# Reordering the first loads of a fused long-convolution and gated-GLU kernel, and fetching D once

## The chip, the cores and the metric

The kernel runs on one core of one Trainium2 chip. The metric is device time in microseconds (us) of one launch; the runs shown are the median of three. Profiles are of one execution on the chip. PE is TensorE's matmul, PEld its weight load, DVE is VectorE, ACT is ScalarE, POOL is GpSimd and SP is SyncE, whose queue issues nearly all DMAs here.

## The reference

x is 2048 tokens by 640 channels in bf16. It is normalised over the channels and goes into two branches that are added to x.

```python
def _A_ref(q, k, v, shift_k, ssm_k, ssm_D):        # q = layernorm(x)
    k_shift = sum over t<4 of k_pad[:, t:t+S, :] * shift_k[:, 3 - t]
    kv = k_shift * v
    y = irfft2(rfft2(kv padded to 2S) * rfft2(ssm_k padded to 2S))[:S]   # causal convolution, 2048 taps
    y = y + kv * ssm_D
    return q * y

def _B_ref(x, w_gate, w_up, w_down):               # x = layernorm(x), F = 1728
    h = sigmoid(x @ w_gate) * (x @ w_up)
    return h @ w_down

x = A_q; xn = _layernorm(x)
return x + _A_ref(xn, A_k, A_v, A_shift_k, A_ssm_k, A_ssm_D) + _B_ref(xn, B_w_gate, B_w_up, B_w_down)
```

## The kernel before

**Branch B** goes over four groups t of 512 tokens. For each, 13 tiles of 128 gate columns and 13 of up columns (`product`, L271), one shared tile for the last 64 columns of each (L292), then the down product (L315) over 14 tiles of hidden rows, in eight pieces of 128 tokens by 320 columns, each in two parts of seven hidden tiles. ACT takes the sigmoid (L280), DVE multiplies (L286) and adds the down product to x (L320). Group 0 is normalised and turned at the very start; its first two gate and up tiles run in quarters (L262).

**Branch A** goes over five chunks c of 128 channels. DVE makes kv from k, the four taps and v (`kv_op`, L348 to L357, in two halves of eight instructions) and turns the filter h with a 32 by 32 transpose (`h_turn`, L334, two instructions a chunk). POOL adds D to the filter's first tap (`add_D`, L328), so that D is part of the convolution. Stage 1 (`st1_mm`, L374 and L376) multiplies kv and h with the table S1 on TensorE; ACT moves the product out of PSUM and SP writes it to DRAM (L392), from where it is read back in another arrangement (L409) for stage 2 (L418), the product of the spectra (L431, L433), and the two inverse stages (L447, L488). DVE multiplies with xn (`inv2_q`, L493, into the tile yx) and adds to x (L498).

**Groups 1 to 3 of x** are normalised while the rest runs: statistics by DVE (`ln_norms`, L200 and L204), the power -1/2 by POOL (L212), then xn by DVE (L217) or ACT (L229), and four DMA transposes by SP (`xn_turn`, L250).

**What sets the order.** Nothing is scheduled automatically after the setup. Each kind of step is a chain of calls, and the string `ORDER` names, letter by letter, which chain makes its next call; so every engine has a fixed list that it works through in order. SP's list begins with the chain "m", a tuple of loads, which the change reorders. Its loads are `load_w` (gate and up columns lo to hi, L177 and L180), `load_wd` (down weights by hidden tile, L186), `ks(c)` (halo and two halves of a chunk's k, L163, L164 and L159), `hs(c)` (`load_h`: D for the chunk, L140, and the filter in four pieces, L143), `vs(c)` (two halves of v, L173), `load_taps` (the tile sraw, L147) and `load_x(1)` (group 1 of x, L133). The table S1 is loaded behind the down weights.

The tile hn that holds a chunk's filter has one buffer: the loads of chunk 1's filter wait until both L334 of chunk 0 have read it. The tile dr for D also has one buffer, so its next load waits for POOL's L328. k has two buffers (`kxs`). Besides what the data need, SP's instruction list has each DMA wait for the landing of an earlier one: completions are counted on eight semaphores in turn, and an issue waits for the DMA that used its semaphore last.

Of the kernel before, what the change touches and what calls it, by code (L numbers as in the profile page):

```python
# [10 lines left out]
BF16 = mybir.dt.bfloat16  # L11
# [3 lines left out]
ALU = mybir.AluOpType  # L15

S = 2048
DM = 640
FF = 1728
P = 128  # L20
# [37 lines left out]
def kernel(  # L58
# [14 lines left out]
    nc = tc.nc  # L73
# [6 lines left out]
    Drow = A_ssm_D.rearrange("(o d) -> o d", o=1)  # L80
# [7 lines left out]
    res = ctx.enter_context(tc.tile_pool(name="res", bufs=1))  # L88
    cv = ctx.enter_context(tc.tile_pool(name="cv", bufs=1))
    dr = ctx.enter_context(tc.tile_pool(name="dr", bufs=1, space=bass.MemoryType.DRAM))  # L90
# [7 lines left out]
    S1t = res.tile([P, NB, 2, P], U16, name="S1t")  # L98
    TBt = res.tile([P, 2, NB, P], U16, name="TBt")
    SMt = res.tile([P, 3, 32], U16, name="SMt")  # L100
    S1 = S1t.bitcast(BF16)
    TB = TBt.bitcast(BF16)
    SM = SMt.bitcast(BF16)
# [21 lines left out]
    sync = nc.sync  # L125
# [3 lines left out]
    cin = [dict() for _ in range(NC)]  # L129
# [5 lines left out]
    def load_h(c):  # L135

        d = cin[c]
        d["hn"] = cv.tile([P, 4, 512], BF16, name="hn")
        d["dr"] = cv.tile([1, P], BF16, name="dr")
        sync.dma_start(d["dr"][:, :], Drow[:, c * P:(c + 1) * P])  # L140
        for q in range(4):
            src = A_ssm_k[c * P:(c + 1) * P, 512 * q:512 * q + 512].rearrange("(k r) t -> r k t", k=4)
            sync.dma_start(d["hn"][32 * q:32 * q + 32, :, :], src)  # L143

    def load_taps(c):
        cin[c]["sraw"] = cv.tile([P, 4 * P], BF16, name="sraw")
        sync.dma_start(cin[c]["sraw"][:], srow[:, 4 * c * P:4 * (c + 1) * P].to_broadcast((P, 4 * P)))  # L147

    def taps(c):
# [175 lines left out]

    def add_D(c):
        h0 = cin[c]["kvh"][0:1, 1, 0:2, :].rearrange("p b c -> p (b c)").rearrange("p (c e) -> p e c", e=2)[:, 0, :]
        nc.gpsimd.tensor_tensor(h0, h0, cin[c]["dr"][:, :], ALU.add)  # L328

    def h_turn(c, n):  # L330

# [27 lines left out]
    chunks = [dict() for _ in range(NC)]  # L359
# [6 lines left out]
    def st1_mm(c, n):  # L366
# [5 lines left out]
        for i in range(4):  # L372
            b = 4 * n4 + i
            nc.tensor.matmul(ps[:, i, 0:P], lhsT=S1[:, b, h, :], rhs=cin[c]["kvh"][:, 0, b, :], start=True, stop=True)  # L374
            hp = cin[c]["kvh"][:, 1, :, :].rearrange("p b c -> p (b c)").rearrange("p (b c e) -> p b e c", b=8, e=2)
            nc.tensor.matmul(ps[:, i, P:2 * P], lhsT=S1[:, b, h, :], rhs=hp[:, b // 2, b % 2, :], start=True, stop=True)  # L376

# [21 lines left out]
    def rd2(s):  # L399
# [5 lines left out]
        else:  # L405
            t2 = (xn[:, 12:NB, :].rearrange("p b d -> p (b d)")[:, 0:2048] if at == 2 else
                  S1[:, 8 * at:8 * at + 8, :, :].rearrange("p b h k -> p (b h k)")).rearrange("p (r e) -> p r e", r=8)
        src = chunks[c]["d1"].rearrange("(r q) h b e -> r (q h b) e", q=NQ)
# [60 lines left out]
    def rdb(c, n):  # L469
# [4 lines left out]
        elif c and n == 1:  # L474
            bi = S1[:, 8:NB, :, :].rearrange("p (h b) s c -> p h (b s) c", h=2)
        else:
# [12 lines left out]
                                 start=(h == 0), stop=(h == 1))  # L489

    def inv2_q(c, m):
        chunks[c]["yx", m] = yx = cv.tile([P, 4, P], BF16, name="yx")
        nc.vector.tensor_tensor(yx[:, :, :], chunks[c]["pb", m][:, :, :], xn[:, 4 * m:4 * m + 4, c * P:(c + 1) * P],  # L493
                                ALU.mult)

# [35 lines left out]
    for i in range(4):  # L531
        m = 3 if i < 3 else NC
# [15 lines left out]
    def step(k, fn, *args):  # L548
        chains[k].append((fn, args))
# [16 lines left out]
    def hs(c):  # L566
        return [(load_h, c)]

    def ks(c):
        return [(load_halo, c), (load_k, c, 0, 8), (load_k, c, 8, NB)]  # L570

    def vs(c):
        return [(load_v, c, 0, 8), (load_v, c, 8, NB)]

    for k in ((load_w, sync, 512, 1024, 0),
              (load_w, sync, 512, 1024, 1),
              (load_taps, 0),
              (sync.dma_start, SMt[:], SMd.ap()),
              (load_w, sync, 1024, 1280, 0),
              (load_w, sync, 1024, 1280, 1),  # L580
              (load_wd, sync, 0, 7),
              *ks(0),
              (load_w, sync, 1280, FF, 0),
              (load_w, sync, 1280, FF, 1),
              *hs(0),
              *vs(0),
              (load_wd, sync, 7, NFC),
              (sync.dma_start, S1t[:], S1d.ap()),
              *hs(1),
              (load_x, sync, 1),  # L590
              *ks(1),
              *vs(1)):
        step("m", *k)
# [4 lines left out]
    for c in range(NC):  # L598
        for n in range(2):
            step("H", h_turn, c, n)  # L600
        step("D", add_D, c)
        for n in range(8):
            step("a", st1_mm, c, n)
# [17 lines left out]
        for m in range(4):  # L621
            step("d", inv2_mm, c, m)
            step("q", inv2_q, c, m)
            step("q", inv2_x, c, m)
        for n in range(16):
            step("k", kv_op, c, n)
        if c == 0:
            continue
        step("T", load_taps, c)
        step("t", taps, c)  # L630
        if c > 1:
# [73 lines left out]
```

## Time and profile before

| | us |
|---|---|
| median of 3 runs (lowest, highest) | 234.59 (233.74, 235.59) |
| the profiled execution: time | 234.78 |
| its span, first to last instruction | 233.0 |
| PE busy | 227.5 (98%) |
| PEld busy | 130.9 (56%) |
| DVE busy | 203.4 (87%) |
| ACT busy | 123.5 (53%) |
| POOL busy | 12.4 (5%) |
| granted TensorE clock | 1.00 |
| DMA | 56.79 MB, mean 244 GB/s |

The span is read from the first to the last instruction; the time of the execution holds 1.78 us more around it. Busy times are sums over the whole span; where an engine waits, and for what, is read from the stretches, the chain of waits and the timeline, which the prediction shows.

### The profile page before, as it was taken

How to read it: one execution, taken by the hardware profiler on the slowest of the kernel's cores; microseconds unless marked ns; L12 is line 12 of the kernel's file. 1: busy time of each engine (PE TensorE's matmuls, PEld its weight loads, DVE VectorE, ACT ScalarE, POOL GpSimd, SP SyncE). 2: the span in 40 equal slices, each digit the busy share in tenths (PEclk: the TensorE clock that was granted, in tenths of full speed). 3: DMA queues.
4: the chain of work that ended last, by engine and by line, in shares of the span. 5: the costliest groups of instructions: out<-in, count | busy, mean ns of one | idle time of the engine just before them, and what ended most of it. 6: DMA issues, size and time to landing. Idle time of an engine off the chain costs nothing.

```text
span 233.0 us, 5431 instructions
## 1 busy us (share of the span) xinstructions
PE 227.5 (98%) x2199; PEld 130.9 (56%) x2200; DVE 203.4 (87%) x357; ACT 123.5 (53%) x158; POOL 12.4 (5%) x26
## 2 busy tenths in 40 slices
PE   7999999997999999999999999999999999999995
PEld 2844446776454555677554544478654544446772
DVE  5444899799999999999999999997799999997773
ACT  2533321676364887765675847674556667752000
POOL 5210010040001100000011000000000000000000
PEclk9999999999999999999999999999999999999999
DMA  6999999896999969999989899689989999364884
GB/s 199 325 329 208 267 317 294 208 266 143 330 221 303 299 221 242 263 223 230 329 237 277 224 319 272 184 217 190 269 210 311 279 263 254 117 169 117 220 266 136
DMA packets 96159, 56.79 MB, mean 244 GB/s; under 512 B 55878, under 2 KB 90374, under 8 KB 95878
## 3 DMA queue, kind: packets, MB, share of 16 engines
q1 hardware_dynamic: 95702, 56.03, 92.6%
q10 hardware_dynamic: 432, 0.41, 0.5%
q8 instruction: 17, 0.28, 0.5%
q14 instruction: 8, 0.07, 0.1%
HBM read 36.12 MB, written 18.35 MB: 234 GB/s over the span
## 4 chain that ended last, share of the span: by engine, by line
PE 87%; DVE 5%; DMA 4%; issue 1%; SPq 1%; ACT 0%; DVEq 0%
PE pu L271 22%; PE pg L271 22%; PE pd L315 21%; PE psb L488 4%; DMA x<-in_A_q_dram 4%; PE ps L374 3%; PE ps L376 3%; PE ps L418 3%; PE psa L447 2%; PE idle L514 2%; PE pg L292 1%; DVE st L200 1%; PE pg L262 1%; PE pu L262 1%; DVE acc L354 1%
## 5 line engine op out<-in xcount | busy, mean ns | idle before, releaser
L271 PEld LDWEIGHTS <-w 128*128 128x128 bf16 x500 | 46.7, 98 | 53.9 <-issue 4.3
L315 PE MATMUL pd<-wd,hT 128*128 128x320 bf16 (+2 forms) x447 | 65.9, 299 | 0.1
L271 PE MATMUL pu<-xnT,w 128*128 128x512 bf16 x250 | 62.2, 379 | 0.0
L271 PE MATMUL pg<-xnT,w 128*128 128x512 bf16 x250 | 62.2, 379 | 0.0
L315 PEld LDWEIGHTS <-hT 128*128 128x128 bf16 x448 | 41.7, 98 | 18.2 <-issue 2.4
L280 ACT ACTIVATE sig<-pg 128x512 bf16<-128x512 f32 x52 | 31.1, 601 | 30.5 <-PE pg L271 23.8
L286 DVE TENSOR_TENSOR hT<-sig,pu 128x512 bf16<-128x512 bf16 x52 | 35.0, 682 | 10.8 <-PE pu L271 6.9
L232 ACT CAST xz<-ps 128x1024 bf16<-128x1024 f32 x36 | 35.1, 1014 | 15.5 <-PE ps L418 15.5
L232 ACT CAST t<-ps 128x1024 bf16<-128x1024 f32 x24 | 23.8, 1012 | 16.7 <-PE ps L376 14.5
L433 DVE TENSOR_TENSOR xz<-xz 128x2048 bf16<-128x2048 bf16 x20 | 24.4, 1221 | 0.2
L374 PE MATMUL ps<-kvh,S1t 128*128 128x128 bf16 x160 | 21.5, 218 | 1.2 <-DVE kvh L357 1.2
L376 PE MATMUL ps<-kvh,S1t 128*128 128x128 bf16 x160 | 21.6, 220 | 0.0
L354 DVE TENSOR_TENSOR acc<-acc,tmp 128x1024 bf16<-128x1024 bf16 x30 | 20.5, 684 | 0.3
L352 DVE TENSOR_TENSOR tmp<-kx,sc 128x1024 bf16<-128x1024 bf16 x30 | 20.5, 682 | 0.3
L320 DVE TENSOR_TENSOR x<-pd,x 128x320 bf16<-128x320 f32 (+2 forms) x32 | 15.2, 484 | 3.8 <-PE pd L315 3.6
L374 PEld LDWEIGHTS <-S1t 128*128 128x128 bf16 x160 | 15.5, 97 | 3.9 <-DVE kvh L357 1.4
L376 PEld LDWEIGHTS <-S1t 128*128 128x128 bf16 x160 | 15.4, 96 | 2.7 <-issue 0.2
L200 DVE BATCH_NORM_STATS2 st<-x 128x6 f32<-128x320 bf16 x32 | 13.8, 473 | 2.3 <-DMA x<-in_A_q_dram 2.3
L232 ACT CAST TBt<-ps 128x1024 bf16<-128x1024 f32 x14 | 13.8, 1012 | 2.7 <-PE ps L376 2.7
L493 DVE TENSOR_TENSOR yx<-psb,xn 128x512 bf16<-128x512 f32 x20 | 13.7, 687 | 1.4 <-PE psb L488 0.8
L431 DVE STREAM_SHUFFLE xz<-xz 128x512 f32<-128x512 f32 x20 | 14.6, 729 | 0.0
L232 ACT CAST ao<-psa 128x1024 bf16<-128x1024 f32 x9 | 9.0, 1013 | 8.6 <-PE psa L447 6.9
(56 smaller groups left out, 159.2 us busy)
## 6 DMA issues: line engine op xcount, KB each, us to landing
t<-d SPq DMA_DIRECT2D x15, 512.0 KB, 6.0
d<-t SPq DMA_DIRECT2D x13, 512.0 KB, 4.1
d<-TBt SPq DMA_DIRECT2D x7, 512.0 KB, 5.9
d<-ao SPq DMA_DIRECT2D x6, 512.0 KB, 5.5
bi<-d SPq DMA_DIRECT2D x6, 512.0 KB, 5.4
kx<-in_A_k_dram SPq DMA_DIRECT2D x10, 256.0 KB, 5.8
hn<-in_A_ssm_k_dram SPq DMA_DIRECT2D x20, 128.0 KB, 5.0
kvh<-in_A_v_dram SPq DMA_DIRECT2D x10, 256.0 KB, 5.2
```

What stands on the lines that cost most here:

```text
L200: nc.vector.bn_stats(st[:, i, SD * s2:SD * s2 + SD], x[:, b, s2 * 320:(s2 + 1) * 320])
L232: nc.scalar.copy(out=out, in_=in_)
L271: nc.tensor.matmul(pg[:, :], lhsT=w[:, c, u * UP + fc * P:u * UP + (fc + 1) * P], rhs=xnT[:, :, c, :], start=(c == 0), stop=(c == NC - 1))
L280: nc.scalar.activation(sig[fc][:, :], pgs[0, fc][:, :], ACT.Sigmoid)
L286: nc.vector.tensor_tensor(hT[:, fc, :], sig[fc][:, :], pgs[1, fc][:, :], ALU.mult)
L315: nc.tensor.matmul(pd[:, :], lhsT=hT[:, fc, bb * P:(bb + 1) * P], rhs=wd[:, fc, es], start=(fc == 0), stop=(fc == NFC - 1))
L320: nc.vector.tensor_tensor(x[:, 4 * t + bb, es], pds[bb, half][:, :], x[:, 4 * t + bb, es], ALU.add)
L352: nc.vector.tensor_tensor(d["tmp"][:, :, :], kx[:, lo + 3 - m:hi + 3 - m, :], sb(m), ALU.mult)
L354: nc.vector.tensor_tensor(d["acc"][:, :, :], d["acc"][:, :, :], d["tmp"][:, :, :], ALU.add)
L374: nc.tensor.matmul(ps[:, i, 0:P], lhsT=S1[:, b, h, :], rhs=cin[c]["kvh"][:, 0, b, :], start=True, stop=True)
L376: nc.tensor.matmul(ps[:, i, P:2 * P], lhsT=S1[:, b, h, :], rhs=hp[:, b // 2, b % 2, :], start=True, stop=True)
L433: nc.vector.tensor_tensor(z[:, 1:3, :, :], z[:, 0:1, :, :].to_broadcast((P, 2, 8, P)), z[:, 1:3, :, :], ALU.mult)
```

## The change

In the chain "m" of SP's loads three things move:

- chunk 0's k (`ks(0)`) goes from behind the first down weights to ahead of the gate and up columns 1024 to 1280;
- the down weights of hidden tiles 0 to 6 go from ahead of k to behind chunk 0's v, next to the other down weights;
- group 1 of x goes ahead of chunk 1's filter loads.

D is loaded once, as one row of 640 values in a tile of its own, ahead of chunk 0's filter, instead of 128 values for each chunk. The tiles sraw and yx share one buffer by a common tag. `ORDER` is the same, and so are all instructions of PE, DVE, ACT and POOL, apart from the tile from which L328 reads D.

```diff
@@ tiles
+    Dt = res.tile([1, DM], BF16, name="Dt")
@@ load_h(c)
         d = cin[c]
+        if c == 0:
+            sync.dma_start(Dt[:, :], Drow[:, :])
         d["hn"] = cv.tile([P, 4, 512], BF16, name="hn")
-        d["dr"] = cv.tile([1, P], BF16, name="dr")
-        sync.dma_start(d["dr"][:, :], Drow[:, c * P:(c + 1) * P])
@@ load_taps(c)
-        cin[c]["sraw"] = cv.tile([P, 4 * P], BF16, name="sraw")
+        cin[c]["sraw"] = cv.tile([P, 4 * P], BF16, name="sraw", tag="sy")
@@ add_D(c)
-        nc.gpsimd.tensor_tensor(h0, h0, cin[c]["dr"][:, :], ALU.add)
+        nc.gpsimd.tensor_tensor(h0, h0, Dt[:, c * P:(c + 1) * P], ALU.add)
@@ inv2_q(c, m)
-        chunks[c]["yx", m] = yx = cv.tile([P, 4, P], BF16, name="yx")
+        chunks[c]["yx", m] = yx = cv.tile([P, 4, P], BF16, name="yx", tag="sy")
@@ chain "m"
               (load_w, sync, 512, 1024, 1),
               (load_taps, 0),
               (sync.dma_start, SMt[:], SMd.ap()),
+              *ks(0),
               (load_w, sync, 1024, 1280, 0),
               (load_w, sync, 1024, 1280, 1),
-              (load_wd, sync, 0, 7),
-              *ks(0),
               (load_w, sync, 1280, FF, 0),
               (load_w, sync, 1280, FF, 1),
               *hs(0),
               *vs(0),
+              (load_wd, sync, 0, 7),
               (load_wd, sync, 7, NFC),
               (sync.dma_start, S1t[:], S1d.ap()),
+              (load_x, sync, 1),
               *hs(1),
-              (load_x, sync, 1),
               *ks(1),
               *vs(1)):
```

## The prediction

> **What bounds the kernel now.** I read first the busy times of the engines in a few long stretches, to find where TensorE stands still, then the chain that ended last around that place, and last the DMA side of it.
>
> The engines' busy time by stretch (stretch, its length, then busy time and instruction count of PE, PEld, DVE, ACT, POOL, the granted clock, the DMA share, GB/s):
>
> ```profile
> 0.00:1.17 1.17, 0.00 (x0) 0.00 (x0) 0.30 (x3) 0.01 (x1) 0.64 (x7) 1.00 0.00 0
> 1.17:54.00 52.83, 52.68 (x389) 31.62 (x389) 38.41 (x74) 21.78 (x34) 7.94 (x15) 1.00 1.06 270
> 54.00:55.24 1.24, 0.04 (x1) 0.00 (x1) 1.21 (x3) 1.01 (x1) 0.00 (x0) 1.00 0.84 161
> 55.24:226.00 170.76, 170.76 (x1781) 96.95 (x1782) 160.31 (x273) 100.65 (x123) 3.83 (x5) 1.00 0.93 242
> 226.00:233.00 7.00, 4.05 (x33) 2.28 (x31) 3.13 (x7) 0.00 (x0) 0.00 (x0) 1.00 0.44 134
> ```
>
> TensorE bounds it, at clock 1.00. Between its first matmul and the drain it is idle once, for 1.20 us just before 55.24; after that it is busy for 170.76 of 170.76 us, in an order fixed at build time. So the end moves one for one with the matmul at 55.24, and a reordering of the first loads can save 1.20 us at the very most.
>
> The chain that ended last (start, length, what), thinned, in order of time:
>
> ```profile
> 31.15 0.65 DVE kvh L357
> ...
> 33.67 0.33 SPq L143
> 34.05 0.42 SPq L143
> ...
> 35.46 8.80 DMA x<-in_A_q_dram
> ...
> 44.29 0.90 DVE st L200 x2
> ...
> 54.49 0.70 DVE kvh L357
> ...
> 55.24 0.23 PE ps L374
> ```
>
> The matmul at 55.24 is chunk 1's first stage-1 product. It waits for DVE's L357, and DVE works without a gap from 44.29 to there: 10.95 us, set off by group 1's x, which was issued at 35.46 and landed at 44.26. x stood behind the four h loads of L143, which SP may issue only when DVE has read chunk 0's h out of the buffer (33.65).
>
> What DVE itself does there (start, length, instruction, idle time before it and what ended it):
>
> ```profile
> 41.15 0.48 DVE L320 TENSOR_TENSOR x<-pd,x 128x320 bf16<-128x320 f32 x1
> 42.79 1.11 DVE L334 STREAM_TRANSPOSE kvh<-hn 128x512 f32<-128x512 f32 x1 [1.15 <-DMA hn<-in_A_ssm_k_dram]
> 44.29 0.49 DVE L200 BATCH_NORM_STATS2 st<-x 128x6 f32<-128x320 bf16 x1 [0.39 <-DMA x<-in_A_q_dram]
> ```
>
> DVE's order is fixed: **h first (L334), then x (L200)**. It was free at 41.64, waited 1.15 us for h and 0.39 us for x: 1.54 us of waiting, more than TensorE's 1.20.
>
> **The change part by part.**
>
> *k and the first down weights.* SP's list has chunk 0's k (two halo loads and two halves, 84 + 11.2 + 2 x 256 KB in the table of issues, whose KB are 1,024 bytes: 622 thousand bytes) ahead of the gate/up columns 1024 to 1280, and the down weights of tiles 0 to 6 behind chunk 0's v. DMA bytes up to S1 stay the same. k moves at the rate of these rows (same columns):
>
> ```profile
> 18.00:21.00 3.00, 3.00 (x15) 1.36 (x14) 0.80 (x2) 0.77 (x2) 0.00 (x0) 1.00 1.26 227
> 21.00:23.00 2.00, 2.00 (x11) 0.88 (x10) 1.43 (x3) 0.60 (x1) 0.00 (x0) 1.00 0.53 116
> 23.00:26.00 3.00, 3.00 (x15) 1.35 (x14) 2.43 (x5) 0.60 (x1) 0.00 (x0) 1.00 1.16 345
> ```
>
> At 227 GB/s that is 2.7 us. The gate columns of 1024 to 1280 were issued at 8.45 and landed 7.9 us later, at 16.35; they come to about 19.1, the up columns to some 20.2. TensorE reads them from its ninth gate tile on: tiles 2, 3, ... start at 11.98 and every 2.16 us, so tile 8 at 24.9. Margin 5.8 us: cost 0. Without that cover, each us late there would stop TensorE for one. Columns 1280 and up, chunk 0's h and v gain what the 1.147 MB of down weights took (3.3 us at 345 GB/s); DVE reads k first at 22.14, after 0.57 us of waiting for it. That wait goes, but at 25.20 DVE waits 0.57 us for TensorE's up tile anyway, so nothing is left of it: 0. The down weights 0 to 6 are read at 36.80. S1, which follows all down weights, landed at 39.95 (issue at 29.85, 10.1 to landing) and takes 1.049 MB / 395 GB/s (the rate of 33 to 36) = 2.7 us; so tiles 7 to 13 are in by 37.3 at the latest, and are read at 38.7; tiles 0 to 6 come 1.065 MB, 2.7 us at that rate, sooner, by 34.6. Cover 2.2 us, cost 0. S1 itself is read at 40.6 against 39.95: 0.6 us of cover, the thinnest; lateness beyond it first eats the 1.20 us that TensorE loses later anyway. Cost 0.
>
> *x ahead of chunk 1's h.* x no longer waits for DVE's 33.65: it is issued right behind S1, from about 30.4. The four h issues still wait for 33.65 and now follow x in the queue, then the taps. The same 1.18 MB of x and h move behind the same S1; only their order is turned, and the one that DVE reads first now comes last. Bound above: the pair ends when it ends today, 44.27. Then L334 starts 0.11 later at 44.38, takes 1.11, and L200 starts at 45.5 instead of 44.29: +1.2 us. Bound below: the pair is in before DVE is free at 41.64; then L200 starts at 42.75, 1.54 sooner, of which TensorE can use 1.20: -1.2. What lies between: h landed at 42.68 today (issue at 34.98, 7.7 to landing), x 1.6 us behind. If h holds today's time though x is ahead of it, L334 keeps 42.79, the 0.39 us wait for x goes, and the gain is 0.4. Two rows speak for a landing before 44.27: the DMA share fell to 0.53 in 21 to 23, so 2.0 x 0.47 = 0.94 us of queue time was lost behind k, which may not recur with other loads there; and h moved slowly (242 GB/s in 36 to 39, beside the tail of S1) where S1 alone had 395. Against: in 41 to 44.3 the mean rate was only 181 GB/s while x still was not in, so a few slow engines of the 16 set the landing, and these need not have lost the 0.94. I take half of the way between 42.68 and 44.27, moved up a little by the last point: h at 43.5. Then L334 at 43.6, L200 at 44.7: **+0.4 us**.
>
> A rule stands beside this. The Trainium skill, DMA: Bandwidth & Descriptors, section "Queues, rings and completion order", says that each DMA engine takes the descriptors of one ring in ring order; what is put ahead on SP's queue is thus paid in full by what is behind. The trace agrees in that x, behind h, landed 1.6 us after it. Strictly by that rule the sum would be the +1.2 of the upper bound, not +0.4.
>
> *Work behind it.* The four statistics feed POOL's L212, L223, L224, then ACT's two L229 (50.46) and SP's four transposes (50.39 to 55.6), read by the gate tile at 58.22. They move with DVE; so does TensorE: 0. k of chunk 1 (L163, L164, L159) is held by the landings of loads eight places ahead in SP's list. The halo no longer waits 2.7 us for S1, but the first half now waits for x to land: from 40.90 to about 42; it took 4.7 us to land, so 46.7, and DVE reads it at 48.34. Cost 0.
>
> *D in one transfer.* Four issues of L140 go (0.23 to 0.44 us of SP each), and the 1.6 us that SP waited at L140 for POOL's L328. SP then still waits for DVE's 33.65, so nothing in front moves. Each issue of SP waits for the landing of the one eight before it, so without four small loads the pairs shift by one to four places for the rest of the run. TensorE has no idle time there and the longest wait of SP is 2.7 us (L163 for S1t); bounds 0 and +2.7, taken as 0, since 170 us without a gap show cover at every load.
>
> *One buffer for taps and yx.* The last read of the taps (L155) ends at 109.5, the first write of yx (L493) is at 145.9: 0.
>
> Sum: 0 + 0 + 0.4 + 0 + 0 = +0.4 us. The profiled execution had a span of 233.0 and a time of 234.78; the three runs shown have a median of 234.59, 0.19 below. Span 233.4; on the median's scale **235.0 us**.
>
> **The rivals.**
>
> *h pays for x in full* (slower). Place: DVE's L334 at 42.79. Price: 1.2 us, worked above: 235.8. It decides from h landing after 43.1, where L334 plus its 1.11 passes 44.29. For it: the fixed DVE order and equal bytes; against it: the 0.94 us hole and the slow stretch. This is also what the skill's ring-order rule would give.
>
> *Both loads are early* (faster). x is queued 5 us sooner, the hole of 21 to 23 is filled, S1's tail is shorter without h beside it: h lands between 41.5 and 42.7, L200 starts 0.4 to 1.54 sooner, gain 0.4 to 1.2. Time 233.4 to 234.2, middle 233.8. Against it: the slow engines in 41 to 44.3.
>
> *A load further on becomes late* through the shifted pairs of SP's waits. Place: SP between 57 and 150, loads of k, v and the stage-2 reads; price: up to the 2.7 us of its longest wait, 237.3. It decides once such a load reaches TensorE after its turn; there is no sign of one, but the trace shows no slack either.
>
> *The change does not do what it says*: x's issue is held by another landing, and all stays in place, 234.6. SP's list shows x waiting only for one of chunk 0's h pieces, long in by then.
>
> **How the numbers follow.** Forecast, h between 42.9 and 44.0: 0.40. h pays in full: 0.21. Both early: 0.24. A later load late: 0.12. No effect: 0.03. One per cent, about what a measurement of this kernel can tell from no change, is 2.35 us: below 232.24 or above 236.94. The largest gain, 1.2, does not reach that; 0.03 for faster, taken from "both early", covers what the runs scatter. Slower is the late load: 0.12. The rest, 0.85, is within 1%. The range takes in full gain (233.4) and full price (235.8), each with some of the scatter of the runs shown (233.74 to 235.59), and reaches just to the late load: 233.0 to 237.2. The forecast's own range is 234.5 to 235.5.
>
> **What would show it.** Right: L200's wait for x gone; L334 waiting about 1.9 us for h; TensorE idle about 1.6 us ahead of its first L374 of chunk 1, and nowhere else before the drain; L348 for chunk 0 starting without a wait for k. Full price: L334 at 44.4 and idle time of 2.4 us. Gain: L334 before 42.8 and idle time under 0.9. Wrong altogether: idle time of TensorE ahead of L271 near 24.9 (gate columns), L315 at 36.8, the first L374 at 40.6 (S1), or anywhere after 60.

## The result, and the profile after

The changed kernel takes 235.21 us (median of 22 runs, 234.16 to 239.01), the kernel before 233.82 us in as many runs beside it (233.54 to 235.59). The ratio is **1.0046, 95% interval 1.0028 to 1.0065**: 1.08 us slower (0.65 to 1.52).

Three of the 22 runs of the changed kernel, the profiled one (238.88 us) among them, show a mean TensorE clock of 0.991 to 0.993 and are left out of the ratio, which is that of the other runs' means (235.18 and 234.10 us) and so smaller than that of the two medians. The lines below are therefore from a second profile of the changed kernel, at clock 1.00 (234.51 us). That one is the fastest of its twelve runs (median 235.44); what a typical run loses has to be read together with the experiments.

Busy time by stretch, changed kernel, second profile (columns as before):

```profile
1.17:54.30 53.13, 52.90 (x389) 31.80 (x389) 38.88 (x75) 21.80 (x34) 7.95 (x15) 1.00 1.06 268
54.30:55.00 0.70, 0.10 (x2) 0.06 (x2) 0.70 (x2) 0.62 (x1) 0.00 (x0) 1.00 1.29 271
55.00:226.00 171.00, 171.00 (x1784) 97.12 (x1785) 160.50 (x273) 101.02 (x124) 3.89 (x5) 1.00 0.94 242
226.00:232.70 6.70, 3.82 (x29) 2.04 (x26) 2.84 (x7) 0.00 (x0) 0.00 (x0) 1.00 0.46 138
```

From 12 us to the drain TensorE is again idle once, 0.60 us at the same matmul, now at 54.94, and busy without a gap after it. The chain that leads there, thinned:

```profile
32.99 1.11 DVE kvh L335
...
35.44 7.43 DMA hn<-in_A_ssm_k_dram
...
43.00 1.11 DVE kvh L335
44.10 0.78 DVE st L201 x2
...
54.19 0.70 DVE kvh L358
...
54.94 0.23 PE ps L375
```

Where x stood, 35.46 to 44.26, there is now h, 35.44 to 42.87. DVE's timeline there says the same:

```profile
41.59 0.48 DVE L321 TENSOR_TENSOR x<-pd,x 128x320 bf16<-128x320 f32 x1
43.00 1.11 DVE L335 STREAM_TRANSPOSE kvh<-hn 128x512 f32<-128x512 f32 x1 [0.92 <-DMA hn<-in_A_ssm_k_dram]
44.03 0.84 DVE L201 BATCH_NORM_STATS2 st<-x 128x6 f32<-128x320 bf16 x2
```

The wait for x is gone and the whole wait is for h. But this run's statistics begin at 44.03, sooner than the 44.29 of the profile before, and its time is below that profile's 234.78. So one profile against one profile would have told a gain. The loss shows only against more runs of both.

### The profile page after: what moved, and what is told of

The parts are those of the page before. It is cut to its first block, busy times and chain, and to the rows that moved or that the text cites. A ratio compares the mean times of both kernels' runs of the same rounds, so it can differ in the third digit from the quotient of the medians.

```text
span 237.1 us, 5426 instructions
## 1 busy us (share of the span) xinstructions
PE 228.8 (97%) x2200; PEld 131.6 (56%) x2200; DVE 203.3 (86%) x357; ACT 123.4 (52%) x158; POOL 12.4 (5%) x26
## 4 chain that ended last, share of the span: by engine, by line
PE 75%; DMA 11%; SPq 8%; DVE 3%; ACT 1%; issue 1%; ACTq 0%
PE pd L316 21%; PE pu L272 18%; PE pg L272 18%; PE psb L489 4%; DMA wd<-in_B_w_down_dram 4%; DMA sraw<-in_A_shift_k_dram 4%; DMA w<-in_B_w_up_dram 3%; PE ps L375 3%; PE ps L377 3%; PE ps L419 3%; PE psa L448 2%; SPq L178 2%; SPq L181 2%; PE pg L293 1%; SPq L160 1%; SPq L187 1%
## 5 line engine op out<-in xcount | busy, mean ns | idle before, releaser
L316 PE MATMUL pd<-wd,hT 128*128 128x320 bf16 (+2 forms) x448 | 67.3, 303 | 0.0
L316 PEld LDWEIGHTS <-hT 128*128 128x128 bf16 x448 | 42.2, 99 | 18.6 <-issue 2.4
L375 PE MATMUL ps<-kvh,S1t 128*128 128x128 bf16 x160 | 21.9, 220 | 2.7 <-DVE kvh L358 2.3
L377 PE MATMUL ps<-kvh,S1t 128*128 128x128 bf16 x160 | 22.0, 222 | 0.0
L335 DVE STREAM_TRANSPOSE kvh<-hn 128x512 f32<-128x512 f32 x10 | 10.9, 1100 | 3.2 <-DMA hn<-in_A_ssm_k_dram 3.2
```

What stands on the lines that cost most here:

```text
L316: nc.tensor.matmul(pd[:, :], lhsT=hT[:, fc, bb * P:(bb + 1) * P], rhs=wd[:, fc, es], start=(fc == 0), stop=(fc == NFC - 1))
```

## The experiments

The ratio is always to the kernel before on the same chip; "idle" is TensorE's idle time between 12 and 58 us in the one profile that came with the run, and the time after it is that profile's own.

| version | ratio (95%) | idle us (time) |
|---|---|---|
| before, second profile | 0.9989 (0.9964 to 1.0014) | 0.13 (233.85) |
| before, third profile | one run | 0.57 (234.23) |
| changed, again | 1.0054 (1.0031 to 1.0078) | 0.60 (234.51) |
| x alone | 1.0023 (1.0009 to 1.0037) | 0.90 (234.92) |
| all but x | 1.0046 (1.0019 to 1.0074) | 1.37 (235.68) |
| k and down weights | 1.0037 (1.0009 to 1.0065) | 1.54 (235.89) |
| D in one transfer | 1.0008 (0.9986 to 1.0031) | 1.14 (235.00) |
| k alone | 1.0052 (1.0028 to 1.0076) | 1.99 (236.21) |
| down weights alone | 1.0029 (1.0002 to 1.0056) | 0.71 (234.20) |
| changed, statistics first | 1.0026 (1.0003 to 1.0050) | 0.77 (234.81) |
| D, S1 in halves | 0.9994 (0.9978 to 1.0010) | 0.00 (234.01) |
| changed, S1 in halves | 1.0063 (1.0039 to 1.0086) | 1.58 (236.05) |

The idle column is not all that differs between two profiles. TensorE's first long gate product (L271; it has other line numbers in some versions) starts anywhere from 11.98 to 12.63 us in these profiles and the first one of before, and that comes before any moved load: the products from the first up product on, at 7.3 to 8.1 us, take a fixed 4.5 to 4.7 us, and the first moved load is issued at 8.58 at the earliest. In all of them the span less this start less the idle time is 219.6 to 220.2 us. So a single profile tells where a version waits, and the ratio tells what it costs.

**The changed kernel again, and x alone.** The first four runs set the step that the prediction made (x in front of h) against the moved k and D. For x alone the edit to the kernel before is

```diff
-              *hs(1),
               (load_x, sync, 1),
+              *hs(1),
```

> The changed kernel once more, for a profile at full clock. Theory A (h, which DVE reads first, now lands last and pays for x in full): ratio about 1.005, L335 of chunk 1 starts near 44.4 after a wait of 2 to 3 us for h, L201 waits 0 for x behind it, TensorE is idle about 2.4 us ahead of its first L375 of chunk 1. Theory B (the loss comes from the moved k and down weights, or from shifted DMA waits further on): L335 near 43, idle time there about 1.2 us as before, and more idle time somewhere else.

> The kernel before with group 1's x ahead of chunk 1's h, and nothing else. Theory A: the whole loss is here, +1.1 us, ratio 1.004 to 1.006, TensorE idle about 2.4 us ahead of chunk 1's first stage-1 product. Theory B: ratio 1.000, idle 1.2 us.

x alone costs 0.54 us (0.21 to 0.87 on 234.04). DVE in that kernel:

```profile
43.37 1.11 DVE L334 STREAM_TRANSPOSE kvh<-hn 128x512 f32<-128x512 f32 x1 [1.22 <-DMA hn<-in_A_ssm_k_dram]
44.40 0.84 DVE L200 BATCH_NORM_STATS2 st<-x 128x6 f32<-128x320 bf16 x2
```

and in the kernel before, second profile:

```profile
41.70 1.10 DVE L334 STREAM_TRANSPOSE kvh<-hn 128x512 f32<-128x512 f32 x1
43.16 0.89 DVE L200 BATCH_NORM_STATS2 st<-x 128x6 f32<-128x320 bf16 x2 [0.36 <-DMA x<-in_A_q_dram]
```

In both, the wait for the last of the pair ends shortly after 43; where it is x, only the statistics wait, and where it is h, its transpose of 1.1 us still stands in between. Theory A holds for the mechanism, not for the size: half of the 1.1 us that it gave. The Trainium skill, DMA: Bandwidth & Descriptors, section "Queues, rings and completion order", has each engine take the descriptors of a ring in order; the trace agrees in the direction, since with x in front only h is waited for.

**All but x.** The changed kernel with the two lines of x and h exchanged back.

> The changed kernel with x back behind chunk 1's h; k, the down weights, D in one transfer and the shared buffer stay changed. Theory A: ratio 0.998 to 1.001, h lands at about 42.7 and TensorE is idle about 1.2 us. Theory B: ratio 1.004 to 1.006, since the parts that cost are still in.

1.0046 is theory B's number: theory A, that x is the whole loss, falls. In its profile DVE waits 1.60 us for h and 0.33 us for x, as in the kernel before's order but later, and TensorE waits 0.41 us for S1 as well.

**Statistics first.** In `ORDER`, the letter H of chunk 1's first transpose moves behind the four l of the statistics:

```diff
-    ...kagaumHglllAKlgAatkw...
+    ...kagaumglllAKlHgAatkw...
```

> The changed kernel with DVE's order made to match the loads: the statistics of group 1 (eight L201, four L205) ahead of chunk 1's first h transpose L335. Theory A: x lands near 42.5, the statistics start there instead of at 45.5, h is in by the time they end; DVE's run starts 1.5 to 2 us sooner than before's 44.29 less the 1.1 us of the transpose, TensorE's idle time falls from 2.4 to 0 to 0.7 us, ratio 0.995 to 0.998. Theory B: ratio stays at 1.004 to 1.006, since the loads are those of the changed kernel.

The ratio falls between the two, 1.0026 (1.0003 to 1.0050), and its interval overlaps those of the changed kernel: that some of the loss comes back is not shown, and there is no gain over the kernel before. The statistics start at 43.23, after 1.01 us of waiting for x, not near 42.5. So matching DVE's order to the loads does not repair the change: the pair itself is late.

**k and the down weights, and D.** The next runs split what was left. k and the first down weights as in the changed kernel, with nothing else; and D in one transfer with the shared buffer, with all loads in the old order.

```diff
-              (load_wd, sync, 0, 7),
-              *ks(0),
+              *ks(0),                # ahead of (load_w, sync, 1024, 1280, 0)
...
+              (load_wd, sync, 0, 7), # behind *vs(0)
```

> The kernel before with chunk 0's k ahead of the columns 1024 to 1280 and the first down weights behind v; D per chunk, x behind h. Theory C (the 256-byte loads of k, now early in SP's list, hold up the loads behind them, so that S1, h and x land later and scatter more): ratio 1.003 to 1.006, idle time of TensorE ahead of chunk 1's first stage-1 product of 1 us or more. Rival D (four small loads fewer shift the waits of SP): ratio 1.000, the loss of the version with all but x is then in D's transfer or the shared buffer.

> The kernel before with D in one transfer and one buffer for taps and yx, all loads in the old order. Theory C: ratio 0.999 to 1.001. Rival D: 1.003 to 1.006, with idle time of TensorE somewhere after 57, or SP waits grown there.

The moved k and down weights cost 0.87 us (0.21 to 1.53 on 234.37), D nothing that shows: the ratios are theory C's, and rival D falls. How the loss reaches TensorE is in the chain that ended last, k and down weights alone, thinned:

```profile
16.70 9.02 DMA w<-in_B_w_up_dram
25.74 0.38 SPq L173
26.17 1.36 SPq L186
27.57 9.19 DMA wd<-in_B_w_down_dram
36.78 0.35 SPq L133
...
37.18 8.67 DMA sraw<-in_A_shift_k_dram
45.95 0.66 ACT sc L155
46.60 0.91 ACT t L232
47.56 0.22 PE ps L374
```

Each DMA here is the one eight places ahead in SP's list, for whose landing the next issue waits: the up columns 1280 to 1664 hold the second half of v, the down weights hold x. SP's longest wait for a landing from 12 to 36, first in this kernel, then in the kernel before (second profile):

```profile
SPq L173 <- DMA w<-in_B_w_up_dram: 2.6, 1, 2.6
```

```profile
SPq L173 <- DMA w<-in_B_w_up_dram: 1.4, 1, 1.4
```

And the DMA engines run low twice (stretches of the same two kernels; the last two numbers are the DMA share and GB/s):

```profile
14.00:18.00 4.00, 4.00 (x20) 1.77 (x19) 1.38 (x2) 1.08 (x2) 0.63 (x1) 1.00 0.94 208
20.00:23.00 3.00, 3.00 (x16) 1.34 (x15) 1.53 (x4) 1.07 (x2) 0.00 (x0) 1.00 1.11 304
26.00:30.00 4.00, 4.00 (x20) 1.85 (x19) 3.79 (x6) 1.19 (x2) 0.00 (x0) 1.00 0.84 167
```

```profile
14.00:18.00 4.00, 4.00 (x21) 1.79 (x19) 1.38 (x2) 0.88 (x3) 0.63 (x1) 1.00 1.08 338
20.00:23.00 3.00, 3.00 (x16) 1.34 (x15) 1.85 (x3) 1.08 (x2) 0.00 (x0) 1.00 0.95 202
26.00:30.00 4.00, 4.00 (x20) 1.80 (x19) 3.64 (x7) 1.19 (x2) 0.00 (x0) 1.00 1.25 205
```

The low stretch moves with k, from 20 to 23 to 14 to 18, and a second one opens at 26 to 30, between v and the down weights, where the kernel before has a share of 1.25. Neither is in every kernel that loses: with k alone, below, the share at 26 to 30 is 1.20, and in the changed kernel's second profile that at 14 to 18 is 1.19.

The chain also shows a second way into TensorE, beside DVE's: the taps of chunk 1 (sraw) come behind the pair, ACT copies them in its fixed order (L155, after a wait of 1.55 us), and an evacuation of stage 1 stands behind that copy. Of TensorE's 1.54 us here, 0.45 us at 47.56 comes this way. The other 1.09 us, ahead of chunk 1, is put down to ACT by the profile, but it is DVE's again:

```profile
55.28 1.01 ACT L232 CAST TBt<-ps 128x1024 bf16<-128x1024 f32 x1 [1.10 <-PE ps L376]
55.58 0.69 DVE L357 TENSOR_TENSOR kvh<-acc,kvh 128x1024 bf16<-128x1024 bf16 x1
56.33 0.10 PEld L374 LDWEIGHTS <-S1t 128*128 128x128 bf16 x1 [1.27 <-DVE kvh L357]
56.33 0.23 PE L374 MATMUL ps<-kvh,S1t 128*128 128x128 bf16 x1 [1.09 <-ACT TBt L232]
```

ACT's copy ends at 56.29 and DVE's L357 at 56.27, and the matmul's own weight load waits for L357. In the second profile of the kernel before the same matmul starts at 54.12, while the same copy of ACT runs from 54.09 to 55.10, so it does not need that copy.

**The kernel before, twice more.**

> The kernel before once more, as a control and for a second profile. Ratio 1.000. The profile shown of before has 234.78 us, 0.7 above the median of 35 later runs: if its idle time of 1.20 us was a slow draw, this profile shows 0 to 0.8 us there and h landed before 42.7; if it is typical, about 1.2 us again.

> A third profile of the kernel before, for the scatter of the landings: same expectation as for the second.

Their idle times are 0.13 and 0.57 us, where the first profile had 1.20. h landed in time or 0.17 us late, x 0.36 and 0.60 us late. The 1.54 us of waiting on which the prediction built were one draw of three, and the longest.

**k alone, and the down weights alone.** k ahead of the columns 1024 to 1280 with the first down weights still between these and the columns 1280; and the first down weights behind v with k where it was.

> The kernel before with chunk 0's k ahead of the columns 1024 to 1280, while the down weights of tiles 0 to 6 stay ahead of the columns 1280 and up; nothing else. Theory E (the loss of the moved loads comes from the down weights: without that long transfer in the queue SP, held by the landing eight loads back, leaves the DMA engines dry at 26 to 30): no idle DMA time at 26 to 30, S1's first engine lands near 36.7, ratio 0.998 to 1.001. Theory F (it comes from k itself, 256-byte pieces early in the list): dry DMA time at 14 to 18 and ratio 1.003 to 1.006.

> The kernel before with the down weights of tiles 0 to 6 behind chunk 0's v; k stays ahead of the columns 1280 and up; nothing else. Theory E: ratio 1.003 to 1.006, dry DMA time ahead of the down weights, S1's first engine lands at 37.5 or later. Theory F: ratio 1.000.

k alone 1.0052: theory E falls, and the cost of k that F expects is there. The down weights alone, 1.0029 (1.0002 to 1.0056), are barely clear of 1, and their profile (0.71 us of idle time) lies among those of the kernel before, so whether they cost anything is open. With k alone the last piece of h for chunk 0 is so late that DVE waits 1.76 us at 32.34 for it, and TensorE stops 0.83 us at the shared tile of L292 and 1.16 us ahead of chunk 1. The DMA share in 14 to 18 is 0.86, against 1.08 in the kernel before.

**S1 in halves.** On the version with D in one transfer and the loads in the old order:

```diff
-              (sync.dma_start, S1t[:], S1d.ap()),
+              (load_S1, 0),          # S1t[:, 0:8]
               *hs(1),
-              (load_x, sync, 1),
+              (load_x_S1,),          # load_x(sync, 1), then S1t[:, 8:16]
```

> D in one transfer with the loads in the old order, and the table S1 loaded in two halves: its blocks 0 to 7 where it stood, blocks 8 to 15 behind group 1's x. 0.52 MB less stand ahead of h and x. If the time goes by the landing of the pair that DVE reads: L335 starts when DVE is free at about 42, L201 at 43 or before, idle time of TensorE ahead of chunk 1's first stage-1 product under 0.3 us, ratio 0.997 to 0.999. If instead the second half of S1 lands after about 44.4, where TensorE reads it, the idle time moves there and the ratio is 1.000 or above.

TensorE in that kernel, from the first long gate product to the last stretch:

```profile
12.50:58.00 45.50, 45.50 (x317) 27.20 (x314) 37.88 (x67) 19.69 (x27) 3.90 (x6) 1.00 1.03 252
58.00:226.00 168.00, 168.00 (x1755) 94.77 (x1753) 157.23 (x269) 98.63 (x121) 3.88 (x5) 1.00 0.93 245
```

No idle time at all; DVE goes from one step to the next with no wait for h or x. The ratio is 0.9994 (0.9978 to 1.0010), its runs lie between 233.63 and 234.26 where those of the kernel before beside them lie between 233.41 and 235.60. It is faster than the changed kernel (the intervals do not touch); against the kernel before it takes away the longer runs, and no gain in the median is shown.

**The changed kernel with S1 in halves.** The last run put the same into the changed kernel, the second half behind chunk 1's h.

> The changed kernel with the table S1 in two halves: blocks 0 to 7 where S1 stood, blocks 8 to 15 behind chunk 1's h; all moved loads stay moved. If the whole loss of the change runs through the landing of h, which DVE waits for ahead of chunk 1: h lands 1.3 us or more sooner, idle time of TensorE ahead of chunk 1's first stage-1 product 0 to 0.4 us, ratio 0.999 to 1.002, with less scatter than the changed kernel's. If the loss sits elsewhere (columns, down weights, waits of SP further on): ratio 1.004 to 1.006, with idle time of TensorE at another place.

1.0063, no better than the changed kernel: the expectation fails. h, now last but for half of S1, is waited for 2.23 us, until 44.48, though 0.52 MB less stand in front of it. TensorE is idle 0.49 us for S1's second half at 45.1, and 1.04 us ahead of chunk 1, where DVE's last step for it (L365 in this version) ends at 56.35 and the matmul starts at 56.41. So the landing of the last loads in the changed order does not go by the bytes in front of them.

**Where the landings come from.** The traces tell more: they record the landing of each of these loads as 16 increments of its semaphore, as many as there are DMA engines, and the load is in with the sixteenth (in the first profile of before h's comes at 42.66 and DVE takes h up at 42.79). The table has the rate of all DMAs from 8 to 30 us, then the times of increments of S1 (its first half where it is split) and of the last piece of chunk 1's filter h.

| profile | GB/s, 8 to 30 | S1: 8th, 15th, 16th | last of h: 8th, 16th |
|---|---|---|---|
| before, first | 277 | 37.18, 37.32, 39.98 | 39.74, 42.66 |
| before, second | 281 | 36.97, 37.48, 39.22 | 39.51, 41.46 |
| before, third | 281 | 37.09, 37.70, 39.73 | 39.68, 41.93 |
| D in one transfer | 277 | 37.35, 37.56, 40.31 | 39.87, 42.60 |
| down weights alone | 274 | 37.13, 37.86, 39.57 | 39.67, 42.04 |
| k alone | 268 | 39.23, 40.63, 41.46 | 42.05, 43.94 |
| k and down weights | 246 | 38.72, 40.63, 41.28 | 41.21, 43.61 |
| all but x | 256 | 37.99, 38.35, 41.64 | 40.53, 43.61 |
| changed, statistics first | 251 | 38.19, 38.55, 39.85 | 42.79, 44.73 |
| changed, again | 277 | 36.74, 37.27, 38.08 | 41.21, 42.88 |
| D, S1 in halves | 280 | 35.74, 35.85, 35.86 | 39.21, 39.94 |
| changed, S1 in halves | 260 | 36.61, 37.11, 39.03 | 41.32, 44.35 |

Two things are told apart here. In the three profiles of the kernel before, fifteen increments of S1 are in by 37.3 to 37.7 and the last comes 1.7 to 2.7 us behind; h shows the same lag (2.0 to 2.9 us), and the idle times of 1.20, 0.57 and 0.13 us follow the last increment of h while the eighth hardly moves. With k in front, the DMA engines have moved less by 30 us and S1 lands later as a whole, in every profile but the changed kernel's second, which is its fastest run. Splitting S1 in the old order took away the lag as well as the bytes. Why less is moved with k in front, for its 256-byte pieces or for SP's waits on earlier landings, and why the last increment lags, no run here tells apart.

## Why the prediction was right or wrong

The median, 235.21, is 0.2 us from the forecast of 235.0 and within 1% of the time before, but that closeness is luck. The forecast put +0.4 us on 234.59, the median of three runs; over 22 runs the kernel before takes 233.82, and the change costs 1.08. A base 0.8 us too high and a change 0.7 us too small cancelled, and the parts of the sum were not those that the runs show.

- *What bounds the kernel.* Right: TensorE, idle between 12 us and the drain only ahead of chunk 1, but for 0.41 us for S1 and 0.10 us behind ScalarE with all but x, 0.45 us behind ScalarE with k and down weights, 0.83 us at L292 with k alone, 0.49 us for S1's second half in the changed kernel with S1 in halves, and pieces under 0.07 us. The 1.20 us at most to be saved was right for that one profile only; the median run of the kernel before has little or nothing to save, as the version without idle time shows, which is 0.06% from it. There was hardly a gain to be had.
- *k and the first down weights, cost 0.* This is the step that failed: 0.87 us (0.21 to 1.53), and k alone is enough for it (1.0052). The covers counted at each reader held for the columns and the down weights; TensorE did not wait for them; the thinnest one, 0.6 us at S1, gave way with all but x (0.41 us of waiting). What was wrong was "DMA bytes up to S1 stay the same", read as "S1 and all behind it land as before". S1 was issued no later (29.19 with k and down weights, 29.71 to 29.85 before), but by 30 us the DMA engines had moved less (246 against 277 to 281 GB/s from 8 us on), and S1's eighth increment came 1.5 to 1.8 us later. The prediction had the 0.94 us of low queue behind k in the old place and counted it as something to win; in the new place more was lost. Its remark that a few slow engines of the 16 set the landing is borne out by the late sixteenth increments.
- *x ahead of h, +0.4.* Measured alone +0.54 (0.21 to 0.87): the size was right within the interval, and so was the sign of the argument, that DVE's fixed order makes h the wrong one to come last. In the changed kernel's second profile the wait for x is gone, as forecast, but h is waited for 0.92 us, not 1.9, and TensorE 0.60 us, not 1.6. The rival "h pays in full" (+1.2) names the place, but x alone does not reach its price.
- *D in one transfer, 0, with up to +2.7 kept open.* Measured +0.2 (-0.3 to +0.7). No TensorE gap after 58 appeared in any profile at full clock; the rival of a later load becoming late did not happen.
- *Work behind the pair.* Missed: ACT's copy of the taps. The taps follow h and x in SP's list, and the copy stands in front of stage 1's evacuations on ACT. Where the pair is late, this can reach TensorE before DVE does, as the 0.45 us at 47.56 with k and down weights shows.
- Summed, the parts measured alone give 0.54 + 0.87 + 0.19 = 1.60 us, together they cost 1.08 and, in the second set of runs, 1.26. Parts that pass through one wait need not add, and the intervals allow either.

## What to carry to other kernels

The order of loads changes not only who comes first but whether the queue stays full. Equal bytes in front of a load do not mean an equal landing: compare what the queue has moved by a fixed time, before and after. When a reader takes its inputs in a fixed order, load them in that order, and look at every engine behind the same stretch of queue, not only at the one that the chain names. Where the profile names the last of several releasers, see when the others ended. An idle time in one profile is one draw: before a gain or a loss is reckoned against it, compare that profile's time with the median over many runs.

## What the runs showed that was not expected

- One kernel, three profiles: idle times of 1.20, 0.57 and 0.07 us ahead of the same matmul, at 234.78, 234.23 and 233.85 us. Between these three the time follows that wait, and the wait follows the last of 16 increments of h.
- Taking half of S1 from in front of the pair removed the wait in one order of loads (idle 0.00) and left it in another (1.58).
